# Linear attention followed by a phase mixer on one core: q's decay always multiplied in at its cast, the decay table of the x copy replaced by buffers, and a new order

## The chip, the cores and the metric

The kernel runs on one core of one Trainium2 chip. The metric is device time in microseconds for one execution, all inputs read from the chip's main memory and the output written back. A core has TensorE (PE; its weight loads are shown as PEld), VectorE (DVE), ScalarE (ACT), GpSimd (POOL) and SyncE (SP, which here only issues DMAs). Each engine works through its own list of instructions in order.

## The reference

Linear attention with a decay per head, over batch 4, 8 heads, 768 tokens and head size 64, and then a mixing layer over tokens and channels (width 512):

```python
gamma = 1.0 - 2.0 ** (-5.0 - np.arange(H, dtype=np.float32))
scale = 1.0 / np.sqrt(D)
for t in range(S):
    state = gamma[None, :, None, None] * state + np.einsum('bhd,bhe->bhde', k[:, :, t], v[:, :, t])
    y[:, :, t] = scale * np.einsum('bhd,bhde->bhe', q[:, :, t], state)
...
x = np.ascontiguousarray(attn_out.transpose(0, 2, 1, 3)).reshape(B, S, H * D)
...
theta = x @ w_theta
zr, zi = x * np.cos(theta), x * np.sin(theta)
y = np.einsum('ts,bsd->btd', w_tok_r, zr) + np.einsum('ts,bsd->btd', w_tok_i, zi)
u = x + y
return (u + np.maximum(u @ w_ch, 0.0)).astype(np.float32)
```

Inputs and output are float32; the matmuls run in bfloat16.

## The kernel before

**The order is written out by hand.** The string ORDER lists some 920 steps as tokens. A token is the name of a function, its numbers and, at the end, a letter for the engine that does it: v VectorE, a ScalarE, p GpSimd; for DMAs s is SyncE's queue and a is ScalarE's. The kernel runs through the string, and each engine gets its instructions in that order; semaphores follow from the tiles.

**Attention by units.** A unit n is 256 tokens of four heads of one batch: n = 2 (3b + i) + h with i the group of 256 tokens and h the half of the heads, 24 units in all. Even and odd units carry separate states. The steps of a unit, in the order of their dependence:

- Lk, Lq, Lv load 256 KB each (line 157), into kqf (for k and q) and vf tiles.
- ck and cq cast k and q to bfloat16 in kqb; cqs casts q and multiplies it by the decay in the same instruction (line 302, table qsc); cv does so for v with the inverse decay (line 308, table vsc).
- Tk and Tq transpose k and q on TensorE (line 316) and E copies the result to kqT; or Dk does all of it as a DMA transpose on SP's queue (line 332).
- A multiplies k by q (line 346), m applies the causal mask on VectorE (line 355), Y multiplies that by v (line 423).
- ST forms the new state's share (line 373), S0 and S1 add up the state for the two chunks of 128 tokens (lines 391 and 395), SB casts it into sbd, and I multiplies q by it (line 411).
- XB copies the unit's result out of PSUM into xT. Where q was cast by cq without its decay, XA does this on VectorE and multiplies by the decay there (line 441, table qx). Two units fill two xT tiles, C = 2 (n // 2) and the next.

**The mixer by tiles of 128 tokens** (six to a batch, 24 in all). For each C: Tx and Ex, or the DMA transpose Dx (line 462), bring x to token order in x_sb; Hh forms theta (line 469); CN takes its sine and its cosine on ScalarE (line 476); z multiplies both by x (line 483). Tw and Ew transpose the token weights once. M.t.s adds the share of z tile s to output tile t (a pair of matmuls, line 509); u adds x; Tu and Eu, or Du (line 531), transpose u; O multiplies it by w_ch (line 536); f takes the maximum with zero, adds u and writes ot (line 542); SO stores ot. The very last tile is done in halves (Mh, uh, Tuh, Euh, Oh, fh, SOh). Z issues two matmuls on zeros, which only keep TensorE at work. y_ps (up to t = 17), th_ps and most o_ps share two PSUM banks named acc.

**The constants.** const2 makes the argument of the decays on GpSimd and VectorE, const3 the tables qsc and vsc on ScalarE; const8 and const9 make the table qx there with eight exponentials (line 233) from what constA prepares on GpSimd; const4 and const5 make the identity and the mask on GpSimd; const7 brings in the sine table.

**Buffers** come from pools: kqf 16, vf 9, xT 4, uT 3, ot 4, z and x_sb 2 for whole batches.

Of the kernel before, what the change touches and what calls it, by code (L numbers as in the profile page):

```python
# [27 lines left out]
S0.2.v S1.2 SB.2.1.a Z.11 cqs.3.p Tq.3 Lv.3.s Tx.0 Tk.3 Z.3 ck.4.p Lv.4.s Lk.5.s Lq.5.s Lv.5.s
Lq.6.s Lk.6.s Lv.6.s Lq.7.s E.3.a SB.2.0.v I.2 Y.2 XB.2.1.a Ex.0.a cv.3.v cq.4.p Tk.4 Lq.8.s A.3
ST.3 Lk.7.s S0.3.v SB.3.0.a S1.3 Lv.7.s Lk.8.s Tx.1 Tq.4 SB.3.1.p cv.4.p m.3 Pw.1.0 XB.2.0.a Ex.1.a  # L30
I.3 Lv.8.s cq.5.a Y.3 E.4.a Pw.0.0 ST.4 Hh.0 ck.5.a cv.5.v CN.0.1 A.4 CN.0.0 S0.4.v Tq.5 Hh.1 Tk.5
XB.3.0.v SB.4.0.p XB.3.1.v SB.4.1.a Pw.0.1 Hh.2 m.4 E.5.v I.4 Y.4 ST.5 ck.6.a Tk.6 Tx.2 cq.6.a
CN.1.1 CN.1.0 XA.4.1 A.5 XA.4.0 m.5 Lq.9.s Ex.2.v S0.5.v z.0.p Tq.6 E.6.a CN.2.0 cv.6.p Hh.3
SB.5.0.v Tx.3 Tw.1.0 z.1.v SB.5.1.a Ew.1.0.v Ex.3.a CN.2.1 A.6 I.5 Y.5 ST.6 XA.5.0 z.2.v Tw.0.0
CN.3.0 Tx.4 CN.3.1 Ew.0.0.v S0.6.v XA.5.1 Ex.4.v Hh.4 CN.4.0 CN.4.1 Tw.0.1 M.0.1 Pw.1.1 z.3.v M.0.0
Tw.0.2 Pw.1.2 Ew.0.2.a SB.6.1.a Hh.5 z.4.p SB.6.0.p Lk.9.a M.0.3 ck.7.p cqs.7.p M.0.2 CN.5.1 CN.5.0
cq.8.a m.6 Ew.0.1.v Tw.1.1 Tw.1.2 Ew.1.1.v Lv.9.s M.0.4 M.1.0 Tx.5 Ew.1.2.v M.1.1 S1.6 Tk.7 M.1.4
Pch Ex.5.v cv.7.p z.5.v Tq.8 Tq.7 M.1.2 M.0.5 I.6 Y.6 ST.7 E.7.v ck.8.a A.7 u.0 S0.7.v m.7 XA.6.1
SB.7.1.a M.1.5 M.1.3 XA.6.0 Tw.1.3 M.2.5 Pw.0.2 M.2.3 u.1 S1.7 Tk.8 M.2.1 M.2.0 SB.7.0.v Ew.1.3.a
Tu.0 I.7 cv.8.p E.8.a cv.9.p Y.7 ST.8 A.8 cqs.9.v ck.9.v M.2.4 Du.1 Lk.10.s Eu.0.a XB.7.1.a XB.7.0.v  # L40
S0.8.v SB.8.0.v M.2.2 Tx.6 Tq.9 Tk.9 Lv.10.a cv.10.p ck.10.p Lq.10.s S1.8 u.2 m.8 O.0 E.9.a SB.8.1.a
Hh.6 Tw.1.4 I.8 Y.8 A.9 CN.6.0 Du.2 Lq.14.s CN.6.1 Ex.6.v f.0 ST.9 Tw.0.3 Hh.7 Ew.1.4.v Ew.0.3.a
S0.9.v Tw.0.4 M.3.0 Tw.1.5 CN.7.0 CN.7.1 M.3.2 Dx.7 M.3.1 M.3.5 M.3.3 Lv.12.s Lk.12.s Ew.1.5.v
XA.8.1 Ew.0.4.v Lq.12.s M.3.4 u.3 S1.9 Tw.0.5 Tk.10 M.4.5 cqs.10.p XA.8.0 m.9 M.4.3 Tq.10 SB.9.1.a
SB.9.0.a I.9 O.2 Lq.11.s Lk.11.s E.10.a Lk.15.s Ew.0.5.v Lk.14.s Y.9 ST.10 A.10 z.7.p Lv.11.s
# [12 lines left out]
SB.14.0.p Lv.16.s Hh.13 S1.14 u.8 Tx.12 M.10.1 cv.15.p cv.17.p SB.14.1.p M.10.0 M.10.4 cqs.18.v
M.10.5 CN.13.0 CN.13.1 Hh.12 CN.12.1 I.14 m.15 Y.14 CN.12.0 ST.15 S0.15.v XB.14.1.a SB.15.0.a M.10.3
cv.16.v Dk.16 Dk.17 Du.7 Dx.13 M.10.2 Dk.18 O.6 SB.15.1.p XB.14.0.v S1.15 I.15 Y.15 ST.16 SO.5.a  # L60
cv.18.p f.6 S0.16.v A.16 M.11.4 SB.16.1.p M.11.1 Lq.21.a Ex.12.a z.12.p SB.16.0.a Lk.19.s Lk.20.s
XB.15.0.a u.10 z.13.p XB.15.1.a m.16 O.7 Du.10 I.16 Y.16 ST.17 f.7 A.17 Tu.8 Hh.15 CN.15.1 CN.15.0
# [571 lines left out]
```

## Time and profile before

| | |
|---|---|
| median of 3 runs | 168.77 us (168.33 to 169.25) |
| the profiled execution | 168.7 us, its span 166.9 us |
| granted TensorE clock | 0.999 |
| matmul busy | 153.7 us, 92% of the span |
| VectorE / ScalarE / GpSimd busy | 114.0 / 78.7 / 76.6 us |
| moved by DMA | 34.93 MB, 209 GB/s on average |
| waits of y_ps matmuls for ot on VectorE | 1.2 us, once |

The span is the time from the first to the last instruction of the profiled execution; the rest of its time lies around it. Each engine's busy time is a sum over its instructions. Matmuls are pipelined, so the duration of one (380 ns for 512 columns) is longer than the distance from one to the next, which the chain shows. In the timeline a line has start, duration, engine, source line, operation, what is written and read, and in brackets the idle time before it with what ended it. In the windows a line has the busy time of PE, PEld, DVE, ACT and POOL, each with its number of instructions, the granted clock, the share of the DMA engines and GB/s.

### The profile page before, as it was taken

What the parts mean: (1) busy time and instruction counts of PE and PEld (TensorE: products, weight loads), DVE (VectorE), ACT (ScalarE), POOL (GpSimd) and SP (SyncE); (2) the same over time, 40 slices, a digit from 0 to 9 for tenths busy, and PEclk for the clock granted to TensorE, in tenths of its full rate; (3) what the DMA queues carried; (4) which work ended last, traced back from release to release, by engine and by line L of the source; (5) the groups of instructions that cost most, each with busy time, mean ns of one, the idle gap of its engine ahead of it and who ended that gap; (6) DMA issues with size and microseconds to landing.
All of it is one profiled execution on the core that took longest, in us unless ns stands there. A gap on an engine that the chain in (4) does not pass through costs nothing.

```text
span 166.9 us, 4887 instructions
## 1 busy us (share of the span) xinstructions
PE 153.7 (92%) x2001; PEld 86.8 (52%) x2030; DVE 114.0 (68%) x210; ACT 78.7 (47%) x141; POOL 76.6 (46%) x110
## 2 busy tenths in 40 slices
PE   5997779998999999999999999969999999999992
PEld 2455546655666556654555555435545544454550
DVE  3298657989994896994779895659868561254462
ACT  4965879981558345763333735822151426000020
POOL 7957369179206642630217699910459303600000
PEclk9999999999999999999999999999999999999999
DMA  4999999999999998949999995999899539414355
GB/s 121 297 290 244 280 282 265 259 227 251 195 197 224 296 184 203 312 102 266 298 301 191 173 245 146 260 215 232 150 216 162 119 64 247 159 61 127 88 211 208
DMA packets 69062, 34.93 MB, mean 209 GB/s; under 512 B 26416, under 2 KB 66096, under 8 KB 69040
## 3 DMA queue, kind: packets, MB, share of 16 engines
q1 hardware_dynamic: 56032, 23.73, 66.9%
q10 hardware_dynamic: 10320, 7.47, 15.5%
q0 software_dynamic: 2688, 3.41, 12.1%
q8 instruction: 16, 0.26, 0.7%
q14 instruction: 6, 0.05, 0.1%
HBM read 25.69 MB, written 6.29 MB: 192 GB/s over the span
## 4 chain that ended last, share of the span: by engine, by line
PE 75%; DMA 11%; ACT 5%; DVE 4%; issue 2%; POOL 2%; DVEq 0%; SPq 0%; POOLq 0%; ACTq 0%
PE y_ps L509 34%; PE o_ps L536 11%; PE th_ps L469 10%; DMA kqf<-in_k_dram 4%; PE r_ps L423 4%; DMA kqf<-in_q_dram 3%; DMA out_dram<-ot 3%; ACT qx L233 3%; PE at_ps L346 3%; PE w_ps L491 3%; PE r_ps L411 2%; PE kq_ps L316 2%; PE y_ps L561 2%; PE x_ps L455 1%; PE r_ps L373 1%
## 5 line engine op out<-in xcount | busy, mean ns | idle before, releaser
L509 PE MATMUL y_ps<-z,wtr 128*128 128x512 bf16 x131 | 49.8, 380 | 2.2 <-DVE ot L542 1.2
L509 PE MATMUL y_ps<-z,wti 128*128 128x512 bf16 x131 | 49.7, 379 | 1.0 <-issue 1.0
L483 POOL TENSOR_TENSOR z<-cs,x_sb 128x1024 bf16<-128x1024 bf16 x12 | 25.4, 2122 | 17.6 <-ACT cs L476 9.8
L355 DVE TENSOR_TENSOR at<-at_ps,mask 128x1024 bf16<-128x1024 f32 x24 | 29.2, 1216 | 0.6 <-PE at_ps L346 0.5
L308 POOL TENSOR_TENSOR vb<-vf,vsc 128x512 bf16<-128x512 f32 x18 | 18.8, 1047 | 21.3 <-DMA vf<-in_v_dram 20.9
L542 DVE SCALAR_TENSOR_TENSOR ot<-o_ps,u 128x512 f32<-128x512 f32 x23 | 15.9, 689 | 15.3 <-PE o_ps L536 12.1
L469 PE MATMUL th_ps<-wth,xT 128*128 128x512 bf16 x88 | 23.9, 380 | 0.5
L516 DVE TENSOR_TENSOR u<-y_ps,x_sb 128x512 bf16<-128x512 f32 x23 | 15.8, 688 | 11.5 <-PE y_ps L509 11.3
L536 PE MATMUL o_ps<-wch,uT 128*128 128x512 bf16 x88 | 23.2, 380 | 0.4 <-issue 0.2
L476 ACT ACTIVATE cs<-th_ps,zerob 128x512 bf16<-128x512 f32 x24 | 16.4, 685 | 13.0 <-PE th_ps L469 8.5
L476 ACT ACTIVATE cs<-th_ps,halfpi 128x512 bf16<-128x512 f32 x24 | 16.3, 685 | 12.9 <-issue 6.8
L139 POOL CAST sbd<-s 64x256 bf16<-64x256 f32 (+1 forms) x21 | 8.9, 423 | 26.9 <-DVE s L391 24.8
L509 PEld LDWEIGHTS <-wti 128*128 128x128 bf16 x138 | 13.5, 98 | 14.2 <-issue 2.5
L509 PEld LDWEIGHTS <-wtr 128*128 128x128 bf16 x138 | 13.4, 97 | 12.8
L137 ACT COPY kqT<-kq_ps 128x1024 bf16<-128x1024 bf16 x11 | 11.1, 1012 | 8.7 <-PE kq_ps L316 8.7
L137 ACT CAST kqb<-kqf 128x512 bf16<-128x512 f32 x17 | 10.3, 619 | 7.7 <-DMA kqf<-in_k_dram 6.0
L469 PEld LDWEIGHTS <-xT 128*128 128x128 bf16 x96 | 8.8, 98 | 8.3
L536 PEld LDWEIGHTS <-uT 128*128 128x128 bf16 x92 | 8.4, 98 | 8.6
L316 PE MATMUL kq_ps<-ident,kqb 128*128 128x128 bf16 x120 | 11.0, 220 | 0.5 <-ACT kqb L137 0.2
L278 PE MATMUL zz<-zero 128*128 128x512 bf16 x27 | 9.3, 477 | 2.0 <-DVE zero L192 1.9
L137 ACT CAST sbd<-s 64x256 bf16<-64x256 f32 (+1 forms) x19 | 6.9, 363 | 8.7 <-DVE s L139 4.0
L423 PE MATMUL r_ps<-at,vb 64*64 64x128 bf16 x384 | 10.0, 221 | 1.0 <-DVE at L355 1.0
(77 smaller groups left out, 207.0 us busy)
## 6 DMA issues: line engine op xcount, KB each, us to landing
vf<-in_v_dram SPq DMA_DIRECT2D x20, 256.0 KB, 5.8
kqf<-in_k_dram SPq DMA_DIRECT2D x19, 256.0 KB, 5.2
kqf<-in_q_dram SPq DMA_DIRECT2D x17, 256.0 KB, 5.0
out_dram<-ot ACTq DMA_DIRECT2D x12, 256.0 KB, 2.9
out_dram<-ot SPq DMA_DIRECT2D x11, 256.0 KB, 3.1
kqf<-in_q_dram ACTq DMA_DIRECT2D x7, 256.0 KB, 5.4
kqf<-in_k_dram ACTq DMA_DIRECT2D x5, 256.0 KB, 4.8
vf<-in_v_dram ACTq DMA_DIRECT2D x4, 256.0 KB, 5.3
```

The lines of the kernel that those rows point to most:

```text
L137: nc.scalar.copy(dst, src)
L308: engines[e].tensor_mul(in_blocks(vb), by_token(raw["vf", n]), _bcast_last(K["vsc"][:, i, :, h * HU:(h + 1) * HU], D))
L316: nc.tensor.transpose(st["kq_ps", n][:, 4 * w + x, :], st["kqb", n][:, w, x * P:(x + 1) * P], K["ident"])
L355: nc.vector.tensor_mul(at.rearrange("p g j a t -> p (g j) (a t)"), st["at_ps", n].rearrange("p g j a t -> p (g j) (a t)"), _bcast_mid(K["m ...
L423: nc.tensor.matmul(st["R", n + 1][c][g * D:(g + 1) * D, j * P:(j + 1) * P], st["vb", n][rows, lo:lo + D], st["at", n][rows, g, j, a, :], s ...
L469: nc.tensor.matmul(th_ps, st["xT", C][:, j, :], K["wth"][:, j, :], start=(j == 0), stop=(j == 3))
L476: nc.scalar.activation(st["cs", C][:, w, :], st["th_ps", C], AF.Sin, bias=K["zerob" if w else "halfpi"], scale=1.0)
L483: engines[e].tensor_mul(st["z", b][:, c], st["cs", C], _bcast_mid(x_of(C), 2))
L509: nc.tensor.matmul(st["y", t], K["wT"][r][:, s0, t0 * P:(t0 + 1) * P], st["z", b][:, s0, r, :], start=(done == 0 and r == 0), stop=(done = ...
L516: nc.vector.tensor_add(st["u", t], st["y", t], st["x", b][:, t0, :])
L536: nc.tensor.matmul(o_ps, st["uT", t][:, j, :], K["wch"][:, j, :], start=(j == 0), stop=(j == nD - 1))
L542: nc.vector.scalar_tensor_tensor(st["ot", t], st["o", t], 0.0, st["u", t], ALU.max, ALU.add)
```

## The change

cq, XA, constA, const8, const9 and the table qx go: every q is cast by cqs with its decay, and every x copy is XB. The SBUF of qx goes to two kqf buffers, one vf, one xT, one uT and two ot. ORDER is laid out anew from end to end. The counts that change: XA 22 to 0, XB 26 to 48; cq 11 to 0, cqs 13 to 24; Tk and Tq 15 to 14, E 15 to 14, Dk 9 to 10; Tx 12 to 10, Ex 12 to 10, Dx 12 to 14; Tu 7 to 6, Eu 7 to 6, Du 16 to 17. Engines change too: z on GpSimd 12 to 5, on VectorE 12 to 19; cqs on VectorE 6 to 14; XB on ScalarE 17 to 28; Ew on ScalarE 3 to 8; stores on ScalarE's queue 12 to 7, loads there 16 to 21. The fifteen Z are the same.

```diff
 ORDER = """
-const2 Lv.0.s const1 const6.v Z.29 Z.2 const5 Z.38 Lk.0.a const3 Z.35 Z.8 Lq.0.s Lv.1.s Z.28 constA
-const4 Lq.1.a cqs.0.v const9 Lk.1.s cv.0.p Z.39 const8 ck.0.p Tk.0 Tq.0 ck.1.a E.0.v Lq.4.a ST.0
-Lk.4.a Z.15 A.0 cqs.1.p Tq.1 Lq.2.s S0.0.v SB.0.1.v Lk.2.s SB.0.0.p cv.1.p Lv.2.s S1.0 I.0 Z.27 m.0
-Tk.1 E.1.a Y.0 ST.1 XB.0.1.a cqs.2.v Z.34 S0.1.v S1.1 cv.2.p SB.1.0.a Pth Lq.3.s Z.18 XB.0.0.v Tq.2
...
+const1 Z.28 Z.15 Z.31 Z.38 const4 const5 Lv.0.s Lk.0.s Z.2 const6.v const2 const3 cv.0.v Lk.2.s
+Lq.3.a Lq.0.s Lv.2.a Lq.4.a Lq.2.s ck.0.a ST.0 Lq.1.s cqs.0.v S0.0.v S1.0 Z.27 SB.0.0.a Lk.1.s
+ck.2.v cqs.1.v cv.2.v SB.0.1.p Tk.2 Tq.0 ck.1.p Tk.0 E.0.a Lk.5.s Z.23 Z.39 Pth const7 A.0 I.0 m.0
+Lk.3.s Lv.1.a Z.3 cqs.3.p Lk.4.s cqs.4.v Tk.1 Tq.1 Z.34 Lv.3.s Lv.4.s Z.18 Z.11 cqs.2.v Tq.2 Y.0
+ck.3.a E.1.a A.1 Tk.3 Lk.6.s XB.0.1.v ck.4.a cv.1.p ST.1 Z.35 Tq.3 Lq.5.s m.1 S0.1.a SB.1.0.p Lv.5.s
+E.2.a SB.1.1.v Pw.0.0 XB.0.0.a S1.1 E.3.a I.1 ck.5.p Y.1 ST.2 S0.2.v Pw.1.0 XB.1.1.a XB.1.0.a A.2
...
+Y.16 ST.17 S0.17.v Hh.15 CN.15.1 CN.15.0 SB.17.0.p XB.16.0.v m.17 XB.16.1.v Dx.15 M.11.0 M.11.1
+Dx.14 SO.3.s M.11.2 M.11.4 Hh.14 SB.17.1.a I.17 u.11 Y.17 ST.18 A.18 z.12.p XB.17.1.v z.15.v CN.14.0
+CN.14.1 Lv.19.a S0.18.a SB.18.1.a O.10 f.10 Hh.17 O.8 XB.17.0.a ck.21.p CN.17.1 CN.17.0 S1.18
+SB.18.0.p Du.9 Dk.19 m.18 f.8 Tu.11 I.18 Dx.17 Eu.11.a Hh.16 z.14.p SO.5.s O.11 CN.16.0 CN.16.1
+cv.20.p Lq.22.a cv.19.v z.17.v Lq.23.a Dx.16 Lv.22.a Y.18 A.19 f.11 ST.19 S0.19.v XB.18.1.a
+SB.19.1.a S1.19 M.12.1 M.12.2 M.12.5 M.12.0 M.13.2 M.13.5 SB.19.0.a XB.18.0.v M.13.3 M.13.0 M.13.1
...
 """.split()
...
-        t = io.tile([P, HU, 2, D], FT, name="vf" if name == "vf" else "kqf", bufs=9 if name == "vf" else 16)
+        t = io.tile([P, HU, 2, D], FT, name="vf" if name == "vf" else "kqf", bufs=10 if name == "vf" else 18)
...
-    def constA():
-        pos = big.tile([P, S], FT, name="pos", tag="z")
...
-    def decay(lo, hi):
-        for x in range(H // 2):
-            nc.scalar.activation(K["qx"][:, x, lo:hi], K["pos"][:, lo:hi], AF.Exp,
-                                 bias=K["lscale"], scale=K["lgp"][:, x:x + 1])
...
-        K["qx"] = const.tile([P, H // 2, S], FT, name="qx")
-
-    def const8():
-        decay(0, 2 * P)
-
-    def const9():
-        decay(2 * P, S)
...
-    def cq(n, e):
-        copy(e, in_blocks(kqb_of(n)[:, 1]), by_token(raw["qf", n]))
...
-            st["xT", C] = work.tile([P, 4, P], BF, name="xT", bufs=4)
+            st["xT", C] = work.tile([P, 4, P], BF, name="xT", bufs=5)
...
-    def XA(n, c):
-        _, i, h = unit(n)
-        nc.vector.tensor_mul(
-            *out_of(n, c),
-            K["qx"][:, 2 * h:2 * h + 2, (2 * i + c) * P:(2 * i + c + 1) * P].rearrange(
-                "p j (t a) -> p j t a", a=2))
...
-        st["uT", t] = work.tile([P, nD, P], BF, name="uT", bufs=3)
+        st["uT", t] = work.tile([P, nD, P], BF, name="uT", bufs=4)
...
-        st["ot", t] = work.tile([P, dm], FT, name="ot", bufs=4)
+        st["ot", t] = work.tile([P, dm], FT, name="ot", bufs=6)
```

More of the change, by code (lines that the diff above doesn't have):

```diff
@@ L28 @@
[L28 to L45, printed above, removed]
@@ L58 @@
[L58 to L62, printed above, removed]
-Dx.14 M.11.2 Tx.15 Lv.22.s M.11.0 M.11.5 S0.17.v SB.17.0.p M.11.3 XA.16.1 m.17 XA.16.0 Ex.15.v Hh.14
@@ L558, in Mh @@
                 st["u", last] = work.tile([P, dm], BF, name="u", bufs=4)
-                st["uT", last] = work.tile([P, nD, P], BF, name="uT", bufs=3)
+                st["uT", last] = work.tile([P, nD, P], BF, name="uT", bufs=4)
         for r in range(2):
```

95 lines of the change are left out of this document (52 added, 43 removed).

## The prediction

> **What bounds the kernel now.** I read the engines' totals first, then the windows of six microseconds, then the chain of waits, and last the timeline of the first 35 us and of 98 to 113 us. The totals and two groups, from the page:
>
> ```profile
> span 166.9 us, 4887 instructions
> PE 153.7 (92%) x2001; PEld 86.8 (52%) x2030; DVE 114.0 (68%) x210; ACT 78.7 (47%) x141; POOL 76.6 (46%) x110
> ...
> L483 POOL TENSOR_TENSOR z<-cs,x_sb 128x1024 bf16<-128x1024 bf16 x12 | 25.4, 2122 | 17.6 <-ACT cs L476 9.8
> L355 DVE TENSOR_TENSOR at<-at_ps,mask 128x1024 bf16<-128x1024 f32 x24 | 29.2, 1216 | 0.6 <-PE at_ps L346 0.5
> ```
>
> TensorE is the bound: 92% of the span. But its busy time holds filler (the zz matmuls of Z), so I count its useful work from the chain, where back-to-back pieces have their true spacing: 0.86 for four 512-column matmuls, 0.22 for four transposes.
>
> ```profile
> 3.95 4.89 ACT qx L233 x8
> 8.85 0.37 ACT kqb L137
> 9.25 6.63 DMA kqf<-in_k_dram
> 15.90 0.37 SPq L157
> 16.31 5.65 DMA kqf<-in_q_dram
> 22.04 0.62 ACT kqb L137
> 22.66 0.92 ACT kqT L137
> ...
> 44.29 0.22 PE kq_ps L316 x4
> 44.51 0.86 PE y_ps L509 x4
> ```
>
> With those prices (and 0.24 for each of A and ST, 0.35 for Y, 0.22 for I, 0.33 for Tw) the order before holds 143.9 us of useful TensorE work. The other 23 us of the span are: 3.6 us after the last matmul (163.3 to 166.9), 4.2 us of idle between 36 and 162 us (summed over the windows), and some 15 us in the start. The chain's first 24 us is a start bound by loads, and its link is the decay table: eight exponentials of qx hold ACT for 4.89 us, so the two loads of unit 4 behind them are issued at 8.77 and 9.25 instead of at 4, and SP's load at 15.90 begins when the second lands. The windows with the idle:
>
> ```profile
> 18.00:24.00 6.00, 4.00 (x112) 2.73 (x102) 2.85 (x6) 4.12 (x10) 2.72 (x5) 1.00 1.20 303
> 36.00:42.00 6.00, 5.27 (x91) 3.47 (x90) 4.92 (x7) 2.15 (x4) 5.88 (x8) 1.00 1.12 249
> 108.00:114.00 6.00, 4.71 (x66) 2.27 (x66) 3.44 (x8) 2.58 (x6) 0.90 (x3) 1.00 1.25 237
> ```
>
> The columns after the length are PE, PEld, DVE, ACT and POOL busy. The last two windows hold one stall each, seen in the timeline:
>
> ```profile
> 38.64 2.02 DVE L483 TENSOR_TENSOR z<-cs,x_sb 128x1024 bf16<-128x1024 bf16 x1
> 40.72 0.38 PE L509 MATMUL y_ps<-z,wtr 128*128 128x512 bf16 x1 [0.68 <-DVE z L483]
> ...
> 110.56 0.69 DVE L542 SCALAR_TENSOR_TENSOR ot<-o_ps,u 128x512 f32<-128x512 f32 x1 [3.05 <-DMA out_dram<-ot]
> 111.30 0.38 PE L509 MATMUL y_ps<-z,wtr 128*128 128x512 bf16 x1 [1.24 <-DVE ot L542]
> ```
>
> At 110.56 the output step f had no free ot buffer; it stood 3.05 us, kept a PSUM bank, and TensorE lost 1.24.
>
> **The change part by part.** The profiled execution took 168.7 us (span 166.9 and 1.8 around it), 0.07 under the median of 168.77; I sum against 168.7.
>
> *TensorE's work.* One unit goes from Tk and Tq to the DMA transpose (Dk 9 to 10), two tiles from Tx to Dx (12 to 14), one from Tu to Du (16 to 17): 8 + 8 + 4 = 20 transposes of 0.055 us less, **-1.1 us**. In a stretch that TensorE bounds this is on the path. The four more DMA transposes cost SP 1.2 us of issue each and land in 3.7 to 5.1 us; the closest consumers, O.21 and O.19, have 0.4 and 0.5 us more TensorE work between the last M and themselves than u (0.69) and 3.8 of landing take. If that cover fails, a late uT costs what its landing is over, 1 to 2 us against the 5.6 of a slow store.
>
> *The casts and copies.* XA and XB cost the same on VectorE (417 and 418 ns), so the table's going saves nothing there; what moves is who does it. On VectorE: 22 XA out (-9.2), XB 9 to 20 (+4.6), cqs 6 to 14 (+8 x 0.68 = 5.4), z 12 to 19 (+7 x 0.68 = 4.8), cv +3 x 0.68, E +3 x 0.69, and Ew, Eu, Ex, ck, cq, S0, SB down by 7.5 together: some +2 us. ACT loses 4.9 of qx and ends about level, POOL loses 17 (z 12 to 5). VectorE stays under TensorE's 143 in sum. Where it lies matters more: cut into slices of 10.3 us of TensorE work, the old order asks VectorE for 14.9, 12.0 and 11.3 us in the first three and for 12.6 in the tenth (around 108 us), all over 10.3; the new one for 17.2, then 9.0, 9.1, and 10.7 at most later. So past the first slice I cost the moves at nothing, hidden by TensorE's work; without that cover, 8 cqs and 7 z at 0.68 are 10 us.
>
> *VectorE beside POOL.* z on VectorE took 0.67 to 0.69 us in eleven of twelve, and 2.02 in the one at 38.64, which ran while POOL did a vb step from 39.05 to 40.11. With 19 z on VectorE and 17 us less on POOL the 0.68 stall at 40.72 may vanish or come elsewhere: **-0.3**, ends -0.7 and 0. The Trainium skill (VectorE: DVE Perf Modes, "Two Vector instructions with no wait between them") says that VectorE's second SBUF read interface is shared with GpSimd and that an operation with two SBUF inputs, as z, reads through it. By that rule alone, seven more z held as the one at 38.64 would put 7 x 1.34 = 9.4 us on VectorE; the one held case agrees, and the other eleven show that it is rare here.
>
> *Output buffers.* ot goes from 4 to 6. The new order needs them: with 4, two f would find every buffer held by a store that comes later in the list. With 6 the tight one is f.11: it waits for SO.5, issued on SP behind Dx.17. From XB.17.1, which frees Dx.17, to f.11 there are 5.3 us of TensorE work; Dx.17's issue (1.2), SO.5's (0.6) and its landing (2.9 median, 5.6 in the bad case) make 4.7 to 7.4, and M.12's four pairs behind f.11 hide another 1.7. So the wait is 0 to 2.1 us on VectorE and 0 to 0.4 on TensorE, or about the old 1.24 if SP is late too. Behind f.11 on VectorE stand S0.19, S1.19, XB.18.0, z.16 and m.19, and I.19, M.12.4 and Y.19 wait for those. I take **-0.8**, ends -1.2 and +0.5.
>
> *Load buffers* (kqf 16 to 18, vf 9 to 10): I see no load that waits for a buffer. What SP's loads wait for is the landing of an earlier one: q3 starts at 7.86 when v1 lands (7.87), v4 at 14.2 when q4 has landed, k5 at 15.90 when k4 has; each time it is the DMA eight places earlier in the list. Zero.
>
> *The start, laid out anew.* POOL does ident and mask (0.58 + 1.49 by the timeline) ahead of const2, so arg comes at 3.5 instead of 1.4, and the exponentials end at 5.5 (1.86 later than they begin). With no qx behind them, ACT issues q3, v2, q4 at about 3.7 and casts k0 by 6.2; ST.0 runs at 6.3 (before: 8.0). But v1, third on SP before, is now issued by ACT behind E.0. E.0 waits for Tk.2, whose cast stands on VectorE behind cqs.0, which needs q0 at 7.0: Tk.0 ends at 9.5, E.0 starts at 9.6, v1 is issued at 9.7 and lands 5.0 to 6.6 later (what the two ACT loads of unit 4 took), at 14.7 to 16.3. cv.1 (1.05) puts ST.1 at about 16.1; before it was at 11.0. By then units 2, 3 and 4 lie ready, so the chain ST, S0, SB, I, Y with m beside it runs at 3.4 us a unit in my walk along the engines' lists (Y.1 17.8, Y.5 31.5), where before it took 4.1 (Y.1 14.2, Y.5 30.7, waiting for q5). The first M comes at 34.0; the old kernel had done the same TensorE work at 33.35. So **+0.65**. Ends: at VectorE's own 2.9 us a unit -1.5; at 4.1 us a unit and a landing of 6.6, +4.7.
>
> Other waits after 36 us: 4.2 - 1.24 - 0.68 = 2.3 us, taken as the same. The last tokens differ little, and the tail stays at 3.6. Sum: 168.7 - 1.1 - 0.3 - 0.8 + 0.65 = 167.15, so **167.1 us**.
>
> **The rivals.** *The start gains.* The chain says that 4.89 us of qx stood in it. If units 1 to 5 run at VectorE's pace, the start term is -1.5 instead of +0.65: 167.1 - 2.15 = 165.0. For it: loads of units 2 to 4 come early. Against it: ST.1 is 5 us later.
>
> *Slower: the late v1.* One load on ACT decides when unit 1's state starts, and units 3 and 5 follow from it. If ACT issues it only after E.0 and const7 have run (1.0 + 1.28 + 0.29), it goes at 12.2, 2.5 us later, and nothing covers that: 169.6; with a landing of 6.6 us, 170.9. It is slower than before from the point where ST.1 starts after 17.7, over half a per cent from 18.6. Against it: at 1.76 ACT issued a load while its table load ran from 1.67 to 2.95, so issue runs ahead of execution. For it: the landing may be longer with SP's six loads in flight.
>
> *A cold TensorE.* The zz matmuls at 1.92 to 6.16 us were 0.43 apart, later ones 0.21 (the granted clock reads 1.00 in both). TensorE has less to do from 7 to 16 us than before (Y.0 at 14.1 instead of 10.8); if it fell back to that pace, ten matmuls would cost 10 x 0.21 = 2.1 us: 169.2. Against it: the old start had waits of 0.9 us and kept the pace. The Trainium skill (TensorE: Matmul & The Clock Gate, "The HAM clock gate") has the array at half clock until some 3.4 us of activity and again after an idle window of that length; the pace of the first zz agrees, no wait here is long enough to show the fall.
>
> *New waits eat the gain.* f.11 waits as f did at 110.56 and z is held by POOL: -0.8 becomes +0.5 and -0.3 becomes 0, and the result is 168.7. That the buffers do not fit can be left out: qx was 12,288 bytes a partition, and the new ones are 4,096 + 2,048 + 1,024 + 1,024 + 4,096 = 12,288.
>
> **How the numbers follow.** Forecast 0.40, start gains 0.16, late v1 0.24, cold 0.05, new waits 0.15. A difference of 0.5%, about what a measurement here can tell, puts the borders at 167.93 and 169.61. Faster: 0.37 of the forecast and all 0.16, 0.53. Same: 0.03 of the forecast, 0.10 of new waits, 0.13. Slower: 0.24 + 0.05 + 0.05, 0.34. The range runs from 164.8, just under the start's gain, to 170.6, short of the late v1 at its worst; the forecast's own is 166.2 to 168.3.
>
> **What would show it.** Right: no qx; ST.1 at 15.5 to 17.5 us; first y_ps at about 34; idle of TensorE from 36 to 162 near 3 us, with no wait of y_ps for ot over 0.5; last matmul at 161 to 162. Wrong: v1 landing after 17, first y_ps after 36, zz or th_ps 0.43 apart after 7 us, or a window past 40 us with TensorE under 5.3 of 6.

## The result, and the profile after

The changed kernel takes **174.8 us** (median of four executions, 173.7 to 175.9) beside 168.7 for the kernel before on the same chip: a ratio of **1.0357, interval 1.0287 to 1.0427**. The forecast was 167.1 with a range of 164.8 to 170.6, so the time lies 4.2 us over the range. Here and below, ratios leave out executions more than 1.5% above the fastest of their kernel; where that takes many away I give the whole spread.

The profiled execution took 175.86 us. From its page:

```profile
span 174.2 us, 4848 instructions
PE 152.7 (88%) x1982; PEld 86.1 (49%) x2010; DVE 117.8 (68%) x203; ACT 73.4 (42%) x142; POOL 61.7 (35%) x95
...
L330 DVE TENSOR_TENSOR at<-at_ps,mask 128x1024 bf16<-128x1024 f32 x24 | 29.2, 1215 | 1.2 <-PE at_ps L321 1.2
...
L451 DVE TENSOR_TENSOR z<-cs,x_sb 128x1024 bf16<-128x1024 bf16 x19 | 15.4, 813 | 8.3 <-DMA x_sb<-xT 5.4
...
L451 POOL TENSOR_TENSOR z<-cs,x_sb 128x1024 bf16<-128x1024 bf16 x5 | 10.7, 2136 | 6.8 <-ACT cs L444 3.4
```

TensorE is busy 1.0 us less than before (152.7 instead of 153.7), and 88% instead of 92% of a span that is 7.3 us longer. VectorE has 3.8 us more, ACT 5.3 and POOL 14.9 less. The mean of z on VectorE is 813 ns, though an undisturbed one takes 680 to 690: a sign that at least one of the 19 was held.

Cut at two points that every kernel here has, the first y_ps and the end of the last o_ps on TensorE, the span is

| | first y_ps at | first y_ps to last o_ps | after it |
|---|---|---|---|
| before | 33.23 | 130.05 | 3.62 |
| forecast | 34.0 | 127.85 | 3.6 |
| after | 38.92 | 129.95 | 5.33 |

Up to the first y_ps both kernels have done about the same useful work on TensorE (16.3 and 16.4 us by the prices of the prediction), so the start alone is 5.7 us later in these two profiles. (Each is of one execution. In the profile of a kernel with the same start and only a store moved at 106 us, the first y_ps comes at 36.09; more of that below.) Windows of six microseconds (length, PE, PEld, DVE, ACT and POOL busy, granted clock, DMA share, GB/s), first three of the kernel before:

```profile
6.00:12.00 6.00, 5.51 (x94) 3.13 (x94) 4.30 (x9) 4.77 (x10) 4.23 (x6) 1.00 1.21 289
12.00:18.00 6.00, 4.86 (x112) 3.29 (x112) 5.25 (x10) 4.21 (x8) 4.22 (x6) 1.00 1.21 239
...
30.00:36.00 6.00, 5.94 (x91) 3.68 (x91) 5.69 (x12) 5.36 (x10) 1.64 (x1) 1.00 1.15 241
```

and of the changed kernel, the start first:

```profile
6.00:12.00 6.00, 3.24 (x53) 1.83 (x54) 3.25 (x8) 2.21 (x4) 0.29 (x1) 1.00 1.15 300
12.00:18.00 6.00, 4.02 (x27) 2.09 (x30) 2.64 (x3) 2.92 (x5) 3.96 (x4) 0.72 1.18 289
18.00:24.00 6.00, 3.24 (x109) 2.38 (x110) 4.14 (x7) 3.34 (x7) 3.73 (x7) 1.00 1.18 266
...
30.00:36.00 6.00, 4.32 (x86) 3.06 (x85) 6.00 (x8) 3.66 (x8) 3.81 (x5) 1.00 1.07 231
36.00:42.00 6.00, 5.60 (x92) 3.72 (x94) 4.76 (x10) 5.44 (x10) 5.73 (x5) 1.00 0.60 143
...
108.00:114.00 6.00, 5.51 (x73) 2.75 (x72) 3.81 (x5) 3.56 (x7) 3.58 (x2) 1.00 0.83 212
114.00:120.00 6.00, 5.00 (x46) 2.37 (x49) 4.46 (x8) 0.59 (x2) 0.00 (x0) 1.00 1.19 300
```

Three things stand here. From 6 to 24 us TensorE has little to do (it is busy for 10.5 us, in the kernel before for 14.4), and in the middle of that the granted clock reads 0.72. From 30 to 36 us VectorE is busy 6.00 of 6 and TensorE waits for it. And the stall around 110 us is not gone but has moved on by some six microseconds. The chain of waits through the start:

```profile
3.76 6.52 DMA kqf<-in_q_dram
...
10.30 3.75 DMA kqf<-in_k_dram
14.05 9.45 DMA wth<-in_moe_w_theta_dram
...
26.26 1.13 DVE at L330
...
30.77 2.96 DVE z L451
33.73 1.13 DVE at L330
```

In this chain loads bound the start until 23.5 us, VectorE's own list from 25.5 to 36.4. The heaviest link of the second part, from the timeline (start, length, engine, line, operation, count, and in brackets the wait before it):

```profile
29.04 1.21 DVE L330 TENSOR_TENSOR at<-at_ps,mask 128x1024 bf16<-128x1024 f32 x1
...
29.34 1.04 POOL L283 TENSOR_TENSOR vb<-vf,vsc 128x512 bf16<-128x512 f32 x1
...
30.77 2.96 DVE L451 TENSOR_TENSOR z<-cs,x_sb 128x1024 bf16<-128x1024 bf16 x1
...
31.12 1.06 POOL L277 TENSOR_TENSOR kqb<-kqf,qsc 128x512 bf16<-128x512 f32 x1
...
32.12 1.05 POOL L283 TENSOR_TENSOR vb<-vf,vsc 128x512 bf16<-128x512 f32 x1
...
33.65 1.21 DVE L330 TENSOR_TENSOR at<-at_ps,mask 128x1024 bf16<-128x1024 f32 x1
...
35.24 0.49 PE L459 MATMUL w_ps<-ident,row 128*128 128x128 bf16 x6 [0.97 <-DVE x_sb L139]
```

z.0 on VectorE takes 2.96 instead of 0.68: it begins just before POOL's cqs.6 and cv.6 and ends only after both. The m step at 29.04, which reads one operand from PSUM, ran beside a POOL multiplication at its usual 1.21. Behind the held z stand m.5, an x_sb and a kqT copy, and TensorE waits for those. Around 114 us:

```profile
114.08 0.69 DVE L451 TENSOR_TENSOR z<-cs,x_sb 128x1024 bf16<-128x1024 bf16 x1 [2.26 <-DMA x_sb<-xT]
...
114.82 0.38 PE L477 MATMUL y_ps<-z,wtr 128*128 128x512 bf16 x1 [1.18 <-DVE z L451]
...
115.27 0.69 DVE L510 SCALAR_TENSOR_TENSOR ot<-o_ps,u 128x512 f32<-128x512 f32 x1 [0.51 <-DMA out_dram<-ot]
```

f.11 waits for an ot buffer only 0.51 here, but z.17 ahead of it waits 2.26 for the DMA transpose Dx.17, and TensorE loses 1.18. The same happens at 149.93 with Dx.22 (1.23).

### The profile page after: what moved, and what is told of

It reads as the page before. It is cut to its first block, busy times and chain, and to the rows that moved or that the text cites. A ratio compares the mean times of both kernels' runs of the same rounds, so it can differ in the third digit from the quotient of the medians.

```text
span 174.2 us, 4848 instructions
## 1 busy us (share of the span) xinstructions
PE 152.7 (88%) x1982; PEld 86.1 (49%) x2010; DVE 117.8 (68%) x203; ACT 73.4 (42%) x142; POOL 61.7 (35%) x95
## 3 DMA queue, kind: packets, MB, share of 16 engines
q0 software_dynamic: 2688, 3.41, 11.4%
## 4 chain that ended last, share of the span: by engine, by line
PE 68%; DMA 16%; DVE 9%; issue 2%; POOL 1%; SPq 0%; DVEq 0%; ACT 0%; POOLq 0%; ACTq 0%
PE y_ps L477 32%; PE o_ps L504 10%; PE th_ps L437 10%; DMA wth<-in_moe_w_theta_dram 5%; DMA kqf<-in_q_dram 4%; PE r_ps L398 3%; PE at_ps L321 3%; DVE at L330 3%; DVE z L451 2%; PE r_ps L386 2%; DMA x_sb<-xT 2%; DMA out_dram<-ot 2%; DMA kqf<-in_k_dram 2%; PE w_ps L459 2%; PE kq_ps L291 2%
## 5 line engine op out<-in xcount | busy, mean ns | idle before, releaser
L477 PE MATMUL y_ps<-z,wti 128*128 128x512 bf16 x134 | 50.8, 379 | 1.2 <-issue 1.0
L477 PE MATMUL y_ps<-z,wtr 128*128 128x512 bf16 x128 | 48.5, 379 | 2.8 <-DVE z L451 2.4
L451 DVE TENSOR_TENSOR z<-cs,x_sb 128x1024 bf16<-128x1024 bf16 x19 | 15.4, 813 | 8.3 <-DMA x_sb<-xT 5.4
L283 POOL TENSOR_TENSOR vb<-vf,vsc 128x512 bf16<-128x512 f32 x15 | 16.2, 1089 | 2.0 <-DMA vf<-in_v_dram 1.7
L137 ACT CAST xT<-r_ps 128x256 bf16<-128x256 f32 x28 | 9.9, 372 | 13.1 <-PE r_ps L348 9.4
L291 PE MATMUL kq_ps<-ident,kqb 128*128 128x128 bf16 x112 | 10.2, 226 | 4.3 <-DVE kqb L139 2.2
L451 POOL TENSOR_TENSOR z<-cs,x_sb 128x1024 bf16<-128x1024 bf16 x5 | 10.7, 2136 | 6.8 <-ACT cs L444 3.4
L139 DVE CAST xT<-r_ps 128x256 bf16<-128x256 f32 x20 | 8.2, 415 | 5.4 <-PE r_ps L398 4.5
L291 PEld LDWEIGHTS <-kqb 128*128 128x128 bf16 x112 | 7.7, 102 | 8.2 <-DVE kqb L139 2.7
L139 POOL CAST kqb<-kqf 128x512 bf16<-128x512 f32 x11 | 7.1, 646 | 13.2 <-issue 9.0
```

The lines of the kernel that those rows point to most:

```text
L137: nc.scalar.copy(dst, src)
L139: engines[e].tensor_copy(dst, src)
L283: engines[e].tensor_mul(in_blocks(vb), by_token(raw["vf", n]), _bcast_last(K["vsc"][:, i, :, h * HU:(h + 1) * HU], D))
L291: nc.tensor.transpose(st["kq_ps", n][:, 4 * w + x, :], st["kqb", n][:, w, x * P:(x + 1) * P], K["ident"])
L451: engines[e].tensor_mul(st["z", b][:, c], st["cs", C], _bcast_mid(x_of(C), 2))
L477: nc.tensor.matmul(st["y", t], K["wT"][r][:, s0, t0 * P:(t0 + 1) * P], st["z", b][:, s0, r, :], start=(done == 0 and r == 0), stop=(done = ...
```

## The experiments

All kernels but the first use the changed code, with its buffers; the edits are to the order. "First y_ps" and "clock" (mean granted) are of each profiled execution; those of the new start with the old rest (179.4 us) and of the old order without 8 fillers (174.3) were the longest of their kernels.

| kernel | median us | ratio (interval) | first y_ps | clock |
|---|---|---|---|---|
| before | 168.7 | 1 | 33.23 | 0.999 |
| after | 174.8 | 1.0357 (1.0287 to 1.0427) | 38.92 | 0.982 |
| old order, new code | 169.1 | 0.9993 (0.9964 to 1.0023) | 32.65 | 1.0 |
| old start, new rest | 171.7 | 1.0128 (1.0081 to 1.0176) | 34.59 | 1.0 |
| new start, old rest | 176.8 | 1.0370 (1.0300 to 1.0441) | 39.13 | 0.971 |
| old order without 8 fillers | 170.8 | 1.0099 (1.0063 to 1.0136) | 33.74 | 0.967 |
| new order with 16 fillers | 174.4 | 1.0330 (1.0263 to 1.0398) | 39.84 | 0.977 |
| the same, z.0 on POOL | 173.3 | 1.0258 (1.0213 to 1.0304) | 36.48 | 0.997 |
| the same, Pw.1.1 earlier | 172.9 | 1.0075 (1.0037 to 1.0112), three of eight | 36.01 | 1.0 |
| old order mended | 168.4 | 0.9959 (0.9930 to 0.9988) | 34.01 | 0.99 |
| old order mended, DMA transposes | 175.5 | 1.0357 (1.0310 to 1.0404) | 34.00 | 0.99 |

### Code or order: four corners

The old order on the new code (before's whole list, with XA written as XB and the five q casts of ACT as cqs on POOL):

```
-XA.0.1.a XA.0.0.a ... cq.n.a const8 const9 constA
+XB.0.1.v XB.0.0.v ... cqs.n.p
 (every other step as before)
```

> The old order from end to end with the new code and buffers (XA as XB on VectorE, cq as cqs, five of them from ScalarE to GpSimd, no qx, constA, const8, const9). If the table's removal is harmless or frees the start (4.89 us of ScalarE in the old chain): 166 to 168.5, first y_ps at or before 33. If doing without it is what costs (casts with decay are dearer, wherever they run): 170 or more, with kq_ps or at_ps waiting for kqb on GpSimd.

It measured 169.1, a ratio of 0.9993. Taken together, the decay always multiplied in, the table's removal, five casts on GpSimd and the new buffers cost and bring nothing that can be measured; the wait for ot is gone. What costs is the order. The two halves of it, joined at the first M:

```
old start, new rest:  [before's list up to its first M] + [what is left of after's list]
new start, old rest:  [after's list up to M.0.0]       + [what is left of before's list]
```

> The changed kernel with the old order's tokens up to the first M in front (XA as XB on VectorE, cq as cqs, those of ScalarE on GpSimd, no qx), and behind them the new order's remaining tokens in the new order. The loss is in the start (5.75 of the 7.3 us of span): first y_ps near 33 us, time 168 to 170. The loss is spread, by VectorE's greater load behind the start and by the tail: first y_ps near 33 but time 172 or more. The removal itself costs the start (casts with decay on GpSimd at 1.04 instead of 0.62 on ScalarE): first y_ps after 36.

> The changed kernel with the new order's tokens up to the first M, and behind them the old order's remaining tokens. Loss in the start: first y_ps near 39 us as in the changed kernel, time 173 to 175 (168.7 + 5.75, tail as before). Loss in the rest and the tail: 170 or less.

They measured 171.7 (+2.5 on the old order) and 176.8 (+7.7), which add up to more than the change lost, so neither is the price of its half alone. In the profile of the second the first y_ps is 6.5 us later than in that of the old order (39.13 against 32.65), and 4.2 us more come between it and the last o_ps (134.92 against 130.68): there a z on VectorE was held beside GpSimd, and the clock was granted at one half from 48.4 to 55.2.

```profile
44.27 4.97 DVE L451 TENSOR_TENSOR z<-cs,x_sb 128x1024 bf16<-128x1024 bf16 x1
```

That most of the loss is in the first 39 us is read from the cut of before and after (5.7 of 7.3 us of span), and both halves agree with it. In the old start with the new rest, TensorE lost 1.42 at 36 to 38 us, at the seam, and 1.4 to a wait for ot at 108 to 114 us.

### The late v1, and the loads as one budget

My rival named v1, third load before and late now. Two kernels take its lateness away. The first issues v1 right behind q0 on SP, and wth at 3.39:

```
 Lk.2.s Lq.3.a Lq.0.s
+Lv.1.s
 ...
-Lk.3.s Lv.1.a        (and Pth moved ahead of SB.0.1.p)
```

> The changed kernel with two tokens moved: v1 is loaded by SP right behind q0, and wth is issued by GpSimd ahead of the casts that wait for k1. If the late v1 and wth make the start: ST.1 by 14 us, no wait of th_ps for wth, first y_ps at 35 to 36, time 170 to 172. If VectorE's load between 25 and 36 us makes it: ST.1 earlier but first y_ps still at 38 or later, time 173 or more.

It took 179.0 (175.9 to 179.4; the profiled execution, the shortest, has the first y_ps at 39.66). Among the waits of its TensorE from 5 to 40 us is this one:

```profile
PE kq_ps L291 <- POOL kqb L139: 3.4, 1, 3.4
```

k1 came later instead, and ST.1 ran at 20.8. The second changes no number of loads: k and v of unit 1 take the places of those of unit 2, and unit 1's steps come forward.

```
-Lk.2.s ... Lv.2.a ... Lk.1.s ck.2.v cv.2.v Tk.2 ck.1.p ... Lv.1.a ... cv.1.p ST.1
+Lk.1.s ... Lv.1.a ... Lk.2.s ck.1.v cv.1.v Tk.1 ck.2.p ... ST.1 ... Lv.2.a ... cv.2.p
```

> The new order, with k and v of unit 1 loaded and cast at the places where those of unit 2 stood and the other way round, and Tk.1, Tq.1, E.1, Y.0, ST.1, A.1, S0.1, S1.1, SB.1.x, m.1 brought forward behind m.0; the number and bytes of the loads are the same. Theory 'unit 1 comes too late': ST.1 at 12 to 13.5 us, first y_ps at 36 to 37.5, 171.5 to 173 us. Rival 'VectorE is the bound from 25 to 36 us whatever came before': ST.1 as early, but first y_ps at 38.5 to 39.5 and 173.5 to 175.5. Rival 'clock': a stretch at 0.5 before 30 us stays, 174 or more.

ST.1 ran at 15.3, 3.5 us earlier, and the kernel took 180.8 (179.2 to 181.7), the slowest of all, with the first y_ps at 45.14. Its timeline (PE and POOL):

```profile
24.78 1.04 POOL L283 TENSOR_TENSOR vb<-vf,vsc 128x512 bf16<-128x512 f32 x1 [7.45 <-DMA vf<-in_v_dram]
...
25.87 0.43 PE L348 MATMUL r_ps<-vb,kqb 64*64 64x64 bf16 x16 [3.53 <-POOL vb L283]
```

Now v2 lands at 24.7. From 6 to 12 us the DMA engines move 289 GB/s in the kernel before and 300 in the changed one, and no window of six microseconds of either has more than 303. I take the loads for one budget: a load brought forward pushes another back, as k1 and v2 were here. "v1 is late" was true, but taking that away made another load late and cost time. Whether some order of the first loads leaves none late was not tried.

### The clock

In the profiles of all eight kernels that have the new start and no added fillers the clock was granted at one half for 3.4 to 13.7 us in all, somewhere between 7 and 31 us. In the profiles of before, of the old order on the new code and of the old start with the new rest it was not; in that of the old order mended, below, it was from 22.5 to 26.0. Is it because TensorE is emptier? Two kernels, one taking fillers from the old order, one putting 16 into the new:

```
old order:  -Z.39 -Z.15 -Z.27 -Z.34 -Z.18 -Z.23 -Z.11 -Z.3
new order:  +5 Z ahead of Tk.2, Z.34 Z.18 Z.11 moved up and +2 Z ahead of Tk.1, +1 Tq.2, +1 A.1,
            +2 ST.1, +2 I.1, +3 Hh.1
```

> The old order on the new code (the kernel of 169.1 us) without eight of its fillers (Z.39, Z.15, Z.27, Z.34, Z.18, Z.23, Z.11, Z.3; 16 matmuls of zz from 8 to 20 us). Theory 'an emptier TensorE is granted half the clock': a stretch of some microseconds at 0.5 between 10 and 30 us in most runs, mean clock 0.95 to 0.985, 170.5 to 173.5 us. Rival 'the fillers do nothing': clock 1.00 and 168.5 to 169.3 us.

> The new order with TensorE's waits in the first 31 us filled: three fillers (Z.34, Z.18, Z.11) moved up and 16 more Z (32 matmuls of zz) put ahead of Tk.2, Tk.1, Tq.2, A.1, ST.1, I.1 and Hh.1. My theory now (the start costs waits of some 4 us and, on top, 1 to 3 us of a clock granted at one half while TensorE has little to do): mean clock 0.995 or more, no stretch at 0.5 before 40 us, first y_ps at 37 to 38.5, 172.5 to 173.7 us. Rival 'the clock is all': first y_ps at 34 to 35, 169 to 170.5. Rival 'the low clock has nothing to do with empty time on TensorE': mean clock 0.96 to 0.98 as before, 175 to 178 us.

Windows of three microseconds in the old order without the eight fillers, and below them two with the fillers:

```profile
12.00:15.00 3.00, 1.67 (x54) 1.16 (x54) 2.85 (x5) 2.53 (x5) 3.00 (x4) 1.00 1.21 290
15.00:18.00 3.00, 1.88 (x36) 1.43 (x36) 2.31 (x5) 1.66 (x3) 1.96 (x3) 0.96 1.17 197
18.00:21.00 3.00, 2.60 (x51) 2.14 (x53) 1.72 (x3) 2.30 (x6) 1.11 (x3) 0.50 1.17 317
...
12.00:15.00 3.00, 2.38 (x47) 1.47 (x45) 2.37 (x5) 2.93 (x7) 3.00 (x4) 1.00 1.20 288
15.00:18.00 3.00, 2.47 (x51) 1.75 (x52) 2.74 (x7) 1.27 (x4) 1.72 (x3) 1.00 1.20 194
```

With TensorE busy 1.67 and 1.88 of 3, the clock falls to 0.50 for 6.8 us; with the fillers the same windows had 2.38 and 2.47, and 1.00 throughout. The kernel is one per cent slower (seven of eight executions from 169.9 to 171.6; the profiled one is the eighth, and in it a z was also held for 4.33 us at 39.65). How much of that is the clock can't be said: executions with a mean clock of 0.992 and 0.996 took 170.8 and 170.2, those at 0.961 to 0.970 169.9 to 171.6. So an emptier TensorE does get half the clock: all eight executions without the fillers have a mean clock under 1.00, and six of the ten with them have 1.00. But in the new order the fillers kept 1.00 up to 36 us and brought next to nothing: 174.4 (173.5 in the one execution with a mean clock of 0.999), and the first y_ps at 39.84. The low clock of the profiled execution came at 36.6 to 40.0 us, after TensorE had waited 1.40 and 0.61, and again at 115.1 to 118.5. I take it that half a clock costs little while TensorE waits for loads and for VectorE anyway.

How the clock falls can be read more closely. Up to 160 us, every stretch at 0.50 in the 20 profiles lasts 3.41 us, or twice or three times that, and where a profile has two stretches their edges lie a whole number of 3.41 us apart, as on a grid of this length. Cut on it, the changed kernel reads:

```profile
10.92:14.33 3.41, 1.19 (x23) 0.66 (x24) 3.13 (x4) 1.93 (x3) 1.22 (x2) 1.00 1.19 288
14.33:17.74 3.41, 3.41 (x18) 1.76 (x15) 0.31 (x1) 2.05 (x3) 2.71 (x3) 0.50 1.18 287
```

In the 13 profiles that have such a stretch, every window of the grid at full clock with TensorE busy for less than 0.45 of it was followed by half the clock (16 windows); of the 20 windows from 0.45 to 0.59 five were. The grid lies elsewhere in each execution: the first fall came at 14.33 here and at 7.58 in the profile of the same start with a store moved. A longer average does not tell: from 18 to 24 us the changed kernel was busy 3.24 of 6, as from 6 to 12, and kept 1.00.

### z.0 between VectorE and POOL

Three earlier kernels moved the fillers alone, z.0 alone, and both with an earlier wth. All three ran under a clock of one half for some microseconds, and none told the causes apart.

```
fillers moved:  Z.34, Z.18 ahead of Tk.2; Z.11 ahead of Z.3
z.0 moved:      -z.0.v  +cqs.6.p z.0.p (cqs.6 brought forward)
both and wth:   and Pth behind SB.0.1.p
```

> The changed kernel with three fillers moved forward: Z.34 and Z.18 from ahead of Tq.2 to ahead of Tk.2, Z.11 to ahead of Tk.1, into TensorE's waits. If the fillers at half pace stand in the start's chain: granted clock 1.00 from 12 to 18 us, Tq.2 at 15 instead of 17.42, ST.1 at 17.8 instead of 18.80, first y_ps 1 us earlier, 173.5. If wth (landing at 23.5) and VectorE set the start: Tq.2 and ST.1 earlier all the same, but th_ps still waits for wth and the first y_ps stays at 38.7 to 39.3, 174 to 175.

> The changed kernel with z.0 on GpSimd instead of VectorE, and cqs.6 put ahead of it there. If VectorE is the start's chain from 26 to 36 us, with 2.96 of it in the one z that GpSimd held: m.5 2 to 3 us earlier, first y_ps at 36 to 37, TensorE over 5 of 6 us from 30 to 36, time 171.5 to 173. If the start is set by loads and a cold TensorE: first y_ps 38.5 or later, 174 to 175.

> Both of the foregoing, and wth issued by GpSimd behind SB.0.1 (about 9 us) instead of behind the cast of k1 (14.05). If fillers, wth and VectorE's held z together make the start: no wait of th_ps for wth, first y_ps at 34.5 to 36, time 170 to 172. If the loads are one budget, as in the run with v1 and wth early, and wth only pushes k3, k4 and v1 back: ST.1 after 18.5, first y_ps as in the run with z.0 alone or later.

They took 178.0 (173.5 to 180.7), 176.0 (174.0 to 176.9) and 175.6 (174.1 to 178.7), the first y_ps at 37.64, 39.42 and 39.22. With the 16 fillers keeping the clock, z.0 was moved again; then the row load Pw.1.1 as well:

```
 (16 fillers)
-z.0.v ... cqs.6.p
+cqs.6.p z.0.p
 (third kernel:) +Pw.1.1 ahead of cv.5.p, -Pw.1.1 behind z.0
```

> The new order with the 16 more fillers of before and with z.0 taken from VectorE to GpSimd behind cqs.6, so that no multiplication of GpSimd runs beside a z on VectorE around 31 us. Theory 'the held z.0 costs the start 2.3 us once the clock is kept': clock 0.99 or more before 34 us, m.5 ends by 33 instead of 34.3 us, first y_ps at 36.5 to 38, 171.5 to 173 us. Rival 'something else arrives as late' (the row loads, wth): first y_ps at 38.5 to 40 and 173.5 to 175 us.

> The same, with the row load Pw.1.1 issued ahead of cv.5 on GpSimd's queue instead of behind z.0. If the row load is what then ends last (it ended a wait of 0.7 us where z.0 was moved alone): first y_ps 0.5 to 1 us earlier than in the kernel with z.0 moved and the fillers, 171 to 172.5 us. If not: the same time within 0.5 us.

The window from 30 to 36 us with the fillers alone, and z.0 and m.5 in it:

```profile
30.00:36.00 6.00, 3.94 (x81) 2.77 (x79) 6.00 (x8) 3.62 (x8) 3.81 (x4) 1.00 1.03 233
...
30.16 2.97 DVE L452 TENSOR_TENSOR z<-cs,x_sb 128x1024 bf16<-128x1024 bf16 x1
...
33.05 1.21 DVE L331 TENSOR_TENSOR at<-at_ps,mask 128x1024 bf16<-128x1024 f32 x1
```

and with z.0 on POOL as well, followed by two lines of that kernel's timeline:

```profile
30.00:36.00 6.00, 5.42 (x131) 4.15 (x129) 4.35 (x10) 5.25 (x11) 5.98 (x5) 1.00 1.01 263
```

```profile
30.49 2.13 POOL L452 TENSOR_TENSOR z<-cs,x_sb 128x1024 bf16<-128x1024 bf16 x1
...
30.52 1.23 DVE L331 TENSOR_TENSOR at<-at_ps,mask 128x1024 bf16<-128x1024 f32 x1 [0.53 <-PE at_ps L322]
```

VectorE falls from 6.00 to 4.35 and now waits for TensorE (0.53), TensorE rises from 3.94 to 5.42. m.5 ends at 31.75 instead of 34.26, 2.5 us earlier, and the first y_ps comes at 36.48 instead of 39.84; what is over 2.5 I put to the half clock that the other profile had from 36.6 to 40.0. The two profiled executions differ as the first y_ps do (172.81 and 176.06), the medians only by 1.1. With the row load earlier, the first y_ps is at 36.01, and three of eight executions took 169.9 to 171.1; the other five took 172.6 to 177.5. So the held z.0 is shown to put m.5 back by 2.5 us in the trace. What that is worth in time is less sure: the medians differ by 1.1, and the executions (173.5 to 176.1 with z.0 on VectorE, 172.7 to 174.6 with it on POOL) overlap.

The loads of an execution move the start as much. In the kernel of the next section that has the changed kernel's start and one store moved at 106 us, z.0 is held for 2.96 as well, and yet the first y_ps is at 36.09: there q0 had landed at 6.7 us instead of 7.7 and wth at 20.2 instead of 23.5, and ST.1 ran at 17.2 instead of 18.8. The rest of the start's loss, 36.0 against 33.2, no edit took away. I put it to the loads, because ST.1 still runs at 18.4 and was at 11.0; that profile speaks for it, but no edit shows it.

### The stall at 108 to 120 us

The prediction named f.11, which waits for the store SO.5 behind Dx.17. The first edit issues SO.5 right behind SO.3, in the mended start and in the changed kernel; the second also puts Dx.17 ahead of Dk.19.

```
 Dx.14 SO.3.s
+SO.5.s
 ...
-SO.5.s            (behind Dx.17)
```

> The new order with the start mended (fillers, z.0 on GpSimd, Pw.1.1 earlier) and the store SO.5 issued right behind SO.3 instead of behind Dx.17. Theory 'f.11 waits for SO.5': no wait of DVE ot for out_dram between 105 and 120 us, idle of TensorE from 102 to 120 us under 1 us, and the scatter of 169.9 to 173.9 us narrows to 168.8 to 170.5. Rival 'Dx.17 alone is late, z.17 waits for it': the wait of f.11 goes, that of z.17 for x_sb (1.3 to 2.3 us) stays and TensorE still loses 1 to 2 us there: 170.5 to 173.

> The changed kernel with nothing but the store SO.5 moved behind SO.3. Its profile lost 1.0 us between 114 and 120 us at this place, others up to 3.4. Theory: 173 to 174.5 us, with no stretch of six microseconds from 102 to 120 under 5.3; the start's 5.7 us and its low clock stay. Rival 'the wait there costs nothing': the same as the changed kernel, 174.5 to 176.

> The same with Dx.17 issued ahead of Dk.19. If z.17's wait for Dx.17 costs TensorE time: z.17 starts 1.2 us earlier and the time falls by 0.5 to 1 us against the kernel with SO.5 alone, to 168.5 to 169.7. If Dk.19 then comes too late for A.19: a wait of at_ps for kqT, and no gain.

They took 172.1 (170.0 to 173.4), 175.5 (172.9 to 181.1) and 175.5 (171.9 to 178.1). From the timeline of the first:

```profile
110.67 0.69 DVE L511 SCALAR_TENSOR_TENSOR ot<-o_ps,u 128x512 f32<-128x512 f32 x1 [2.68 <-DMA out_dram<-ot]
...
111.41 1.76 PE L505 MATMUL o_ps<-wch,uT 128*128 128x512 bf16 x4 [2.24 <-DVE ot L511]
...
114.44 0.69 DVE L452 TENSOR_TENSOR z<-cs,x_sb 128x1024 bf16<-128x1024 bf16 x1 [2.49 <-DMA x_sb<-xT]
...
115.05 0.68 DVE L511 SCALAR_TENSOR_TENSOR ot<-o_ps,u 128x512 f32<-128x512 f32 x1
```

The profiled execution took 173.3, near the longest of its six. f.11 (115.05) waits no more, as the theory said; but f.8 (110.67), the output step before it, waits 2.68 for a store instead, by the list SO.3, which SP issued at 104.59, and z.17 waits 2.49. The clock then read 0.50 from 111.6 to 115.0. With Dx.17 ahead of Dk.19, z.17 waited 0.38 and TensorE 1.4 for kqT. Each edit moved the wait to the neighbour: between 97 and 118 us SP's queue is one list of transposes, stores and loads that is busy nearly without a gap, and in each of these three profiles something in it came late. In the profiles of kernels with the new rest TensorE idles 0.2 to 4.3 us from 108 to 120 us, in that of the changed kernel 1.5. I take this scatter for what spreads the executions of the mended start at a clock of 1.00; it could not be removed here.

### The old order mended

Its own three waits (row_i 0.97, z.5 held by a POOL cv 0.85, SB.18 0.72) gave:

```
+Pw.1.1 ahead of z.0.p   +Pw.0.2 ahead of cv.7.p   ck.21.p behind SB.18.1.p
```

> The old order with the new code and buffers, and three moves on GpSimd for the waits that this order has with them: the row load Pw.1.1 ahead of z.0 (w_ps waited 0.97 for it), Pw.0.2 ahead of cv.7 (which held z.5 on VectorE, y_ps waited 0.85), ck.21 behind SB.18.1 (r_ps waited 0.72). If those waits are time: 1.5 to 2.5 us under the old order with the new code, 166.5 to 167.6, faster than before. If TensorE only waits elsewhere instead: 168.5 to 169.3.

168.4, a ratio of 0.9959 (0.9930 to 0.9988): a little under the kernel before, and the best version here, though not the 166.5 to 167.6 that the three waits promised. Five more fillers:

> The mended old order (two row loads ahead of the POOL steps that held them, one cast of k behind SB.18.1) with five more Z ahead of I.2, I.3, Y.3 and ST.4, where TensorE waited 0.35 to 0.87 us and the clock was seen at 0.63 and 0.51. If the fillers keep the clock at 1.00 and lie in the waits: first y_ps at 32.5 to 33.2, 167.6 to 168.4 us. If they only take time (10 matmuls of 0.21): 169 to 170 us.

168.8, 0.9990 (0.9960 to 1.0019): not better. Then the term of my sum that held, fewer transposes on TensorE, alone in the mended old order:

```
-Tk.19 Tq.19 E.19.a   +Dk.19      -Tx.12/15/17 Ex.12/15/17   +Dx.12/15/17      -Tu.4/8 Eu.4/8   +Du.4/8
```

> The mended old order (168.4 us) with the change's shift of transposes from TensorE to the DMA and nothing else of the new order: Tk and Tq of unit 19, Tx of 12, 15, 17 and Tu of 4 and 8 become DMA transposes, 28 transposes of 0.055 us less on TensorE, 1.5 us. If the term of the sum holds wherever TensorE is the bound: 166.8 to 167.3 us. If the DMA transposes come late and their consumers wait: 168 us or more, with a wait on kqT, x_sb or uT for DMA in the list of waits.

It took 175.5, seven microseconds *more*. The first y_ps is unmoved (34.00); from there to the last o_ps it needs 134.5 instead of 129.8. From its timeline:

```profile
98.84 1.89 PE L504 MATMUL o_ps<-wch,uT 128*128 128x512 bf16 x4 [1.54 <-DMA uT<-u]
```

Two waits of at_ps for DMA transposes of kqT (1.1) and chains of small waits behind them follow, and half the clock from 98.7 to 102.1. I conclude that the 1.5 us saved on TensorE are real only where the list around them lets the DMA transposes come in time.

## Why the prediction was wrong, step by step

**Transposes, -1.1.** Right in size: 19 matmul records fewer, 1.0 us by the price used. The reason was thinner than I wrote: I checked two consumers and priced the issue on SP at nothing. In the old order the same kind of shift cost seven microseconds.

**Casts, copies, SBUF: nothing.** Right in time: 0.9993. (ACT, which I had about level, has 5.3 us less to do.)

**z held by POOL, -0.3 with ends -0.7 and 0.** This step failed. I saw the one held z (2.02) and counted it as a stall that might go; I did not look where the new z on VectorE stand beside POOL's multiplications. z.0 at 30.77 is one such place, held 2.96 and at the head of VectorE's list. The Trainium skill (VectorE: DVE Perf Modes, "Two Vector instructions with no wait between them") says that an operation with two SBUF inputs uses the read interface shared with GpSimd. The runs agree as far as they go: m with its PSUM operand was never held, and a z on VectorE could be. But it was not held each time: of the z behind which a GpSimd multiplication began within 0.24 to 0.41 us, nine stood 2.02 us or more, and in thirteen z took 0.77 or 0.78 and the multiplication was the longer one (1.36 or 1.37 instead of 1.05). In the nine, GpSimd was issuing a DMA as z began, at z.0 the row load Pw.1.1; in the thirteen it was not. My reading of that rule, seven held z at once, was as wrong as my zero: one was enough.

**Output buffers, -0.8.** The wait of y_ps for ot went from 1.24 to 0.18, as said, and f.11's wait was 0.51 of my 0 to 2.1. But I had Dx.17 on the path of SO.5 and not on that of z.17, which it feeds: y_ps waited 2.4 for z in two places. By difference, the waits after the first y_ps rose by some 0.9 instead of falling by 1.1, so the middle is 129.95 and not 127.85.

**The start, +0.65 with ends -1.5 and +4.7.** This is the step that failed most: it was +5.7 by TensorE's work, over even the upper end. Step by step: q0 landed at 7.7, not 7.0, so the kqT copy E.0 started at 10.26, not 9.6; v1 was issued at 11.20, not 9.7, since ACT issued it 0.9 us after that start and not 0.1; it landed at 16.7, not 14.7 to 16.3. ST.1 ran at 18.80 and not 16.1: cv.1 was done at 17.77, but in front of ST.1 on TensorE stood Tk.1, waiting for k1 (cast by POOL only at 13.11), six fillers at the pace of a half clock (2.77 us for six) and Tq.2 at 17.42. From Y.1 (21.11) to Y.4 (30.50) units took 3.1 us, a little better than my 3.4. The last, to Y.5, took 6.2, because of z.0. Against my walk, then, Y.1 came 3.3 us late, the next three units gave back 0.8, and the last lost 2.8. The walk also left out wth: it was issued at 14.05 (12.51 before) and landed 9.5 us later, and th_ps waited 1.67 for it. I had counted VectorE's first slice at 17.2 us of work over 10.3 of TensorE's and then walked the units at 3.4 us each without carrying that excess to its end.

**The rivals.** The start did not gain by losing qx: without it the old order's first y_ps came 0.6 us earlier (32.65) and its time stayed the same, so the 4.89 us in the old chain were not worth that. The late v1 had the right sign and its threshold was passed (ST.1 after 17.7), but its price, 169.6 to 170.9, was too small, and bringing v1 forward cost time, so that v1 alone is not shown to be the cause. The cold TensorE, at 0.05, came true as an event. The Trainium skill (TensorE: Matmul & The Clock Gate, "The HAM clock gate") has two states only, full and half, and the fall after an idle window of some 3.4 us; the clock here does read 0.50, for 3.41 us at a time, but the window before the fall was not idle: TensorE was busy for 1.19 of its 3.41 us, and no single gap in it was above 2.0. I dismissed this rival because no wait was long enough, where a window with several waits in it was. Its price was small in the new order (174.8, with the fillers 174.4) and at most 1.7 us in the old one.

**The tail, 3.6.** It measured 5.3, with the last stores landing in 3.2 to 3.7 us instead of 1.8. Twelve of the 20 profiled executions have 3.6 to 4.1 us there, and eight have 4.8 to 5.3, with the last stores landing in 2.9 to 3.7 us instead of 1.8 to 2.4. The eight are the changed kernel and six with its start and rest nearly as they are, and the old order without eight fillers; the new rest behind the old start, or with 16 fillers more, is among the twelve. I can't put it down to the order, and its cause stays open.

Together: by the profiled execution the changed kernel is 8.7 us over the forecast, 4.9 of them up to the first y_ps, 2.1 from there to the last o_ps and 1.7 in the tail. The range was too narrow by my own terms as well: with the start at its upper end the sum gives 171.2, and I closed the range at 170.6.

What stays open beside it: which of the transfers between 97 and 118 us has to go for that stall to end; the 3 us of the start that I put to the order of the first loads; and whether moving Pw.1.1 alone, with z.0 left on VectorE, would have freed z.0.
